# Expert routing by remainders of integer keys, with a running maximum and ids in half precision

## The chip, the cores and the metric

The kernel runs on one core of a Trainium2 chip. The time is that of the device in microseconds (us). The engines are TensorE (PE; its weight loads are PEld), VectorE (DVE), ScalarE (ACT), GpSimd (POOL) and SyncE (SP, which here issues transfers). Each takes its own list of instructions, and a semaphore makes one wait for another. PSUM is the memory that TensorE writes, in eight banks.

## The reference

Three layers follow each other. (1) Attention over windows of 64 positions, 4 batches of 8 heads, 576 positions, head size 64. Its output is x, 2304 tokens of 512. (2) A mixture of 8 experts in which every expert takes exactly 288 tokens:

```
logits = x @ w_gate                       # 2304 x 8
for idx in argsort(-logits.flatten()):    # best (token, expert) pair first
    tok, e = idx // 8, idx % 8
    if assigned[tok] >= 0 or counts[e] >= 288: continue
    assigned[tok] = e; counts[e] += 1
out[mask] = relu(x[mask] @ w1[e]) @ w2[e]  # mask = assigned == e
```

(3) Two dense layers, 512 to 2048 and back, with a leaky relu between them. The result has 2304 rows of 512.

## The kernel before

**Order of the work.** All instructions are issued in program order on each engine; nothing reorders them. attention() runs 18 steps of 128 tokens. Beside it, filler() and ahead() put pieces of other work between the steps. Then Moe.run() goes through experts 0 and 1, the dense layers for the first 512 tokens ("m" 0), experts 2 and 3, "m" 1, and so on. The weights of the dense layers come packed, and Convert unpacks them on ScalarE and VectorE up to the end of "m" 0. RouteDriver.tick() puts routing and conversion pieces between the matmuls: the class Clocks keeps a modelled time for each engine, and a piece is issued when its model says that its inputs are there.

**The routing.** The greedy loop is done in eight phases. In each phase every free token looks at its best open expert, and the phase finds the value at which the first expert becomes full (the threshold). Tokens above it are assigned, and that expert is closed. Its 288 token ids then go to an indirect gather of the rows of x. Phase 0 lies between the end of attention and expert 0; phase p+1 runs beside the work of the experts before it.

**The search in one phase.** A threshold is found in 6 rounds, of 127 candidates (the upper bits of the float32 pattern) and then of 31 (5 bits each). In each round VectorE compares the 18 columns of token maxima m with the candidates T (the grid, GE, in self.G), TensorE counts the hits by expert (18 matmuls of 8 columns into a PSUM tile pc), VectorE compares the counts with what each expert can still take (r_sat), and one matmul with powers of two (pow2) sums the candidates passed. A maximum over experts (r_ns) gives the digit. Then integer instructions put it onto the threshold so far (r_fb) and make the next table of candidates (r_U, r_T). In phase 0, grid and counts are cut into columns 0 to 8 and 9 to 17, and the grid of round 0 has been made by ahead() during attention.

**From threshold to ids.** A scan counts tokens in each expert's order (S), a matmul adds the counts of the other partitions, and each token gets a slot. One-hot tables of slot // 16 (r_OB, three blocks: times column number, times partition number, plain) and slot % 16 (r_lo) are multiplied by 18 matmuls. r_ip spreads the product, and a last float32 product with cf['comb'] gives the ids of 3 x 96 tokens (r_ids). The expert's number (r_eidx) is known earlier, and SP loads its weights with it.

**Where the constants come from.** cft (float32) is loaded on ScalarE's queue at the start, by early(). cbt has two parts: its first 128 columns (an identity) come on ScalarE's queue too; the rest, with the tables tri, iota, cont and spread, is loaded by late() on SP's queue, with cit (integers) ahead of it. late() then calls Router.start(), which sets the routing's state on VectorE.

**PSUM.** attention's pool a_ps has the tags "as" (two buffers of two banks, scores), "apt" and "ao". values() puts the outputs of the last two steps into "as" buffers. After attention the pools m_pa (4 buffers of one bank, tag "acc"), rps (one buffer, all small tiles of the routing), pm and m_ph are opened in this order. The last three steps' outputs are scaled by ScalarE, eight instructions a step (line 185).

Lines: 336 to 339 start(), 354 to 368 ahead(), 137 maxima, 145 exponentials, 152 copies of transposes, 165 values, 1374 and 1375 the loads of late(). Instructions issued after attention all show line 1230, a helper's, so tiles tell them apart.

Of the kernel before, what the change touches and what calls it, by code (L numbers as in the profile page):

```python
# [17 lines left out]
NT = 18  # L18
# [254 lines left out]
U32 = mybir.dt.uint32  # L273
# [3 lines left out]

def consts_np():
# [9 lines left out]
    f['lim'] = np.where(p == 0, -1.0, 3e9).astype(np.float32)  # L288
    f['cid'] = np.broadcast_to(np.arange(18, dtype=np.float32), (128, 18))
    f['pid'] = np.broadcast_to(p, (128, 1))  # L290
# [7 lines left out]
    b['cont'] = np.broadcast_to((np.arange(288) % NT > 0).astype(np.float32), (128, 288))  # L298
    b['spread'] = (j % 6 == np.arange(96) // 16).astype(np.float32)
# [11 lines left out]
class Router:  # L311
# [3 lines left out]
    def __init__(self, nc, pool, pp, L, cf, ci, cb, ones_b, pow2):  # L315
# [6 lines left out]
        self.rem = pool.tile([128, 8], F32, name="r_rem")  # L322
        self.rem0 = pool.tile([128, 8], F32, name="r_rem0")
# [3 lines left out]
        self.OB = pool.tile([128, 1048], BF, name="r_OB")  # L327
        for x in self.G + [self.OB]:
            nc.gpsimd.memset(x, 0.0)
        self.ip = pool.tile([128, 128], F32, name="r_ip")  # L330
    def start(self):
        v, cf = self.nc.vector, self.cf
        v.memset(self.base, 0.0)
        v.memset(self.sat, 0.0)
        v.memset(self.ip, 0.0)
        v.tensor_copy(self.uw, cf['ew'])
        v.memset(self.slotg, 0.0)
        v.memset(self.rem, 288.0)
        v.tensor_scalar(out=self.rem0, in0=self.rem, scalar1=cf['lim'], scalar2=None, op0=ALU.min)
    def ps(self, p, n):  # L340

        self.nps += 1
        return self.pp.tile([128, 128], F32, tag="rp", name=f"rp{self.nps}")[:p, :n]
    def t(self, shape, dt, name, ph):
        bufs = {"fb": 2, "ns": 2, "T": 2, "U": 2, "ids": 8, "eidx": 8}.get(name, 1)
        return self.pool.tile(shape, dt, tag="r_" + name, name=f"r_{name}_{ph}", bufs=bufs)
    def ahead(self, a, b):

        v = self.nc.vector
        if a == 0:  # L350
            self.first = [self.t([128, NT], F32, "m", 0), self.t([128, NT, 8], BF, "oh", 0), self.t([128, NT], F32, "mxw", 0)]
            self.ge0, self.win0 = self.grid(0, 128)
            self.eqw0 = self.G[1].bitcast(F32)[:, :8 * NT].rearrange("p (c e) -> p c e", e=8)
# [15 lines left out]
    def grid(self, k, w):
# [3 lines left out]
    def phase(self, ph, out):  # L373
# [25 lines left out]
        theta = None  # L399
        if ph < 7:  # L400
            fb = ns = U = None
            T = ci['t1']
            for r in range(6):
# [4 lines left out]
                pc = None  # L408
                for lo, hi in () if ph + r == 0 else ((0, 9), (9, 18)) if J > 32 or ph == 0 else ((0, 18),):
                    w = hi - lo  # L410
                    TT(out=GE[:, lo:hi, :J], in0=b3(m[:, lo:hi], w, J), in1=bm(T.bitcast(F32), w, J), op=ALU.is_ge)
                    if hi == 9:
                        yield 'p' if ph == 0 else 'd', 0
                        if ph == 0:
                            pc = self.ps(128, 8)
                            for c in range(9):
                                nc.tensor.matmul(pc, win(c), OH[:, c, :], start=(c == 0), stop=False)
                if r >= 2:
                    nf = t([128, 1], I32, "fb", f"{ph}_{r}")
                    TT(out=nf, in0=fb, in1=ns, op=ALU.bitwise_xor)  # L420
                    fb = nf
                if 1 <= r <= 4:
                    Jn = NB[r]
                    U = t([128, 32], I32, "U", f"{ph}_{r}")
                    TT(out=U[:, :Jn], in0=ci[f'jt{r}'], in1=fb.to_broadcast([128, Jn]), op=ALU.bitwise_xor)
                yield 'p', 0
                c0 = 9 if pc is not None else 0
                pc = self.ps(128, 8) if pc is None else pc
                for c in range(c0, NT):
                    nc.tensor.matmul(pc, win(c), OH[:, c, :], start=(c == 0), stop=(c == NT - 1))  # L430
# [8 lines left out]
                if r == 0:  # L439
                    k = t([128, 2], I32, "k", ph)  # L440
                    TS(out=k[:, 0:1], in0=ns, scalar1=1, scalar2=None, op0=ALU.logical_shift_left)
                    TS(out=k[:, 1:2], in0=k[:, 0:1], scalar1=31, scalar2=0x7FFFFFFF, op0=ALU.arith_shift_right, op1=ALU.bitwise_and)
                    fb = t([128, 1], I32, "fb", f"{ph}_{r}")
                    STT(out=fb, in0=k[:, 0:1], scalar=-1, in1=k[:, 1:2], op0=ALU.bitwise_xor, op1=ALU.bitwise_xor)
                    T = t([128, 31], I32, "T", f"{ph}_{r}")[:, :NB[0]]
                    TT(out=T, in0=ci['jt0'], in1=fb.to_broadcast([128, NB[0]]), op=ALU.bitwise_xor)
                elif r < 5:
                    T = t([128, 31], I32, "T", f"{ph}_{r}")[:, :NB[r]]
                    TT(out=T, in0=U[:, :NB[r]], in1=ns.to_broadcast([128, NB[r]]), op=ALU.bitwise_xor)
                else:  # L450
                    nf = t([128, 1], I32, "fb", f"{ph}_{r}x")
                    TT(out=nf, in0=fb, in1=ns, op=ALU.bitwise_xor)
                    theta = nf.bitcast(F32)
        ge = t([128, 2, NT], F32, "gteq", ph)
        gt, eq = ge[:, 0], ge[:, 1]
        if theta is not None:
            TS(out=gt, in0=m, scalar1=theta, scalar2=None, op0=ALU.is_gt)
            TS(out=eq, in0=m, scalar1=theta, scalar2=None, op0=ALU.is_equal)
# [9 lines left out]
        S = self.OB.bitcast(F32)[:, :16 * NT].rearrange("p (k e c) -> p k e c", k=2, e=8)  # L468
# [947 lines left out]
```

## Time and profile before

| | |
|---|---|
| median of 3 runs | 773.43 us (772.1 to 773.63) |
| the profiled execution's own time | 779.16 us |
| its span, first to last instruction | 777.5 us |
| TensorE busy | 736.7 us (95%) |
| VectorE busy | 448.9 us (58%) |
| ScalarE busy | 335.0 us (43%) |
| GpSimd busy | 169.1 us (22%) |
| DMA | 138.55 MB, mean 178 GB/s |
| mean granted TensorE clock | 0.978 |

In a row of a timeline the first number is the start in us from the span's start, the second the duration, then engine, line, operation, output<-inputs, sizes, and in brackets how long the engine had stood idle and what ended that. TensorE has two clock levels, 1.2 and 2.4 GHz; a granted clock of 1.00 is the upper one. Busy time of PE is no measure of its speed.

### The profile page before, as it was taken

Reading aid. Unit: us, or ns where it says so; the run is one execution under the profiler, and the core shown is the slowest. Engines: PE = TensorE matmul, PEld = TensorE weight load, DVE = VectorE, ACT = ScalarE, POOL = GpSimd, SP = SyncE. Lnnn points to the kernel's source line nnn. Section 1 sums busy time; section 2 is a strip of 40 time slices with the busy share of each in tenths; the row PEclk is TensorE's granted clock in tenths of the full one; section 3 lists DMA queues with packets and bytes.
Section 4 is the critical chain, followed back from the end, with each engine's and each line's share of the span. In section 5 each row is a group of like instructions: output and inputs, shape, how many; then the busy total and the mean of one; then the engine's idle time right before and its main releaser. Section 6 shows DMA issues by size and latency. Waiting matters only on the chain.

```text
span 777.5 us, 15224 instructions
## 1 busy us (share of the span) xinstructions
PE 736.7 (95%) x5872; PEld 625.8 (80%) x5872; DVE 448.9 (58%) x1204; ACT 335.0 (43%) x736; POOL 169.1 (22%) x255
## 2 busy tenths in 40 slices
PE   6999559999999989999999999999999999999996
PEld 4777437798867879997778899988889998888895
DVE  3798778998888978977677324322233222222332
ACT  5898707786645443522112445322244532221321
POOL 5253030400100032120000497200028840000201
PEclk9999769999999999999999999999999999999998
DMA  9996156833883755462144265623436462324752
GB/s 349 408 413 265 46 177 233 299 92 129 265 262 127 254 181 167 138 216 83 55 158 145 81 213 166 220 58 132 163 97 217 152 217 82 108 63 172 253 171 99
DMA packets 39943, 138.55 MB, mean 178 GB/s; under 512 B 4926, under 2 KB 5822, under 8 KB 39872
## 3 DMA queue, kind: packets, MB, share of 16 engines
q1 hardware_dynamic: 35136, 123.19, 45.9%
q0 software_dynamic: 4304, 14.16, 5.3%
q8 instruction: 46, 0.75, 0.4%
q10 hardware_dynamic: 432, 0.25, 0.1%
q14 instruction: 25, 0.20, 0.1%
HBM read 117.65 MB, written 19.92 MB: 177 GB/s over the span
## 4 chain that ended last, share of the span: by engine, by line
PE 83%; DVE 7%; DMA 5%; ACT 2%; issue 1%; another core or an unknown queue 0%; POOLq 0%; POOL 0%; ACTq 0%; SPq 0%; DVEq 0%
PE h L1230 37%; PE oa L1230 24%; PE ya L1230 13%; PE rp L1230 4%; DMA cv_in<-in_wio_dram 2%; PE ao L165 2%; DMA aq<-in_q_dram 1%; DMA avt<-in_vt_dram 1%; PE apt L150 1%; PE xtp L1230 1%; DVE r_G L1230 1%; PE as L130 1%; PE warm L1230 1%; DMA cft<-in_cf_dram 1%; DVE w L1230 1%
## 5 line engine op out<-in xcount | busy, mean ns | idle before, releaser
L1230 PE MATMUL oa<-w,hh 128*128 128x512 f32 x540 | 135.2, 396 | 0.0
L1230 PE MATMUL h<-Y,w 128*128 128x512 f32 (+1 forms) x600 | 134.3, 371 | 0.0
L1230 DVE SCALAR_TENSOR_TENSOR h<-h,tg 128x512 f32<-128x512 f32 (+1 forms) x80 | 51.5, 644 | 133.5 <-ACT tg L1230 131.7
L1230 ACT COPY tg<-h 128x512 f32<-128x512 f32 (+1 forms) x80 | 43.4, 543 | 190.7 <-PE h L1230 185.8
L1230 PEld LDWEIGHTS h<-Y,w 128*128 128x128 f32 x600 | 104.4, 188 | 18.8
L1230 PEld LDWEIGHTS oa<-w,hh 128*128 128x128 f32 x540 | 100.8, 190 | 20.6 <-ACT hh L1230 0.2
L1230 POOL TENSOR_TENSOR w<-raw,w 128x512 fp32r<-128x512 f32 x53 | 66.7, 1292 | 197.1 <-DVE xT L1230 100.8
L1230 PE MATMUL h<-xT,w 128*128 128x288 f32 x672 | 101.5, 299 | 0.0
L1230 PE MATMUL ya<-hh,w 128*128 128x288 f32 x672 | 101.0, 298 | 0.0
L1230 PEld LDWEIGHTS h<-xT,w 128*128 128x128 f32 x672 | 93.2, 189 | 3.0 <-issue 2.4
L1230 PEld LDWEIGHTS ya<-hh,w 128*128 128x128 f32 x672 | 92.8, 190 | 0.3 <-DVE hh L1230 0.2
L1230 PE MATMUL h<-Y,res 128*128 128x512 f32 (+1 forms) x360 | 82.9, 375 | 0.0
L1230 PE MATMUL oa<-res,hh 128*128 128x512 f32 x324 | 82.5, 398 | 0.0
L1230 DVE TENSOR_TENSOR hh<-h,hh 128x512 fp32r<-128x512 f32 (+1 forms) x80 | 50.9, 637 | 38.0 <-ACT hh L1230 37.3
L1230 PEld LDWEIGHTS h<-Y,res 128*128 128x128 f32 x360 | 62.6, 188 | 12.0
L1230 ACT CAST hh<-h 128x512 fp32r<-128x512 f32 (+1 forms) x80 | 43.5, 544 | 64.8 <-DVE h L1230 64.3
L1230 PEld LDWEIGHTS oa<-res,hh 128*128 128x128 f32 x324 | 59.2, 188 | 13.2 <-ACT hh L1230 0.4
L1230 POOL DMA_INDIRECT out_dram<-ot,sidx x18 | 19.2, 1069 | 226.4 <-DVE ot L1230 223.4
L1230 ACT ACTIVATE hh<-h 128x288 fp32r<-128x288 f32 (+1 forms) x64 | 26.5, 414 | 95.3 <-PE h L1230 91.3
L1230 ACT CAST w<-raw 128x512 fp32r<-128x512 f32 x112 | 64.0, 619 | 0.1
L1230 DVE SCALAR_TENSOR_TENSOR hh<-h,hh 128x288 fp32r<-128x288 f32 x56 | 25.4, 453 | 63.9 <-ACT hh L1230 58.9
L145 ACT ACTIVATE ap<-as,anm 128x128 f32<-128x128 f32 x144 | 41.8, 403 | 17.5 <-PE as L130 7.8
(164 smaller groups left out, 933.1 us busy)
## 6 DMA issues: line engine op xcount, KB each, us to landing
w<-wsp SPq DMA_DIRECT2D x80, 512.0 KB, 3.7
raw<-in_w_dram SPq DMA_DIRECT2D x53, 512.0 KB, 3.9
cv_in<-in_wio_dram SPq DMA_DIRECT2D x32, 512.0 KB, 4.4
wsp<-w SPq DMA_DIRECT2D x20, 512.0 KB, 3.1
avo<-in_v_dram SPq DMA_DIRECT2D x6, 876.0 KB, 10.1
aq<-in_q_dram SPq DMA_DIRECT2D x12, 384.0 KB
avt<-in_vt_dram SPq DMA_DIRECT2D x6, 768.0 KB, 9.0
xd<-ax SPq DMA_DIRECT2D x18, 256.0 KB, 7.9
```

What stands on the lines that cost most here:

```text
L130: nc.tensor.matmul(S[64 * t:64 * t + 64, a, u, :].rearrange("p (b c) -> p b c", b=2), q[h], k[h], start=False, stop=True, skip_group_check ...
L145: nc.scalar.activation(p[:, u, :], S[:, a, u, :], AF.Exp, bias=nm[a][:, u:u + 1], scale=0.125)
L150: nc.tensor.transpose(pt[:, u, :], p[:, u, :], ident)
L165: nc.tensor.matmul(o[64 * t:64 * t + 64, h // 4, h % 4, :], ptb[:, u, 64 * t:64 * t + 64], (ve, vo)[t][m][:, s, h, :], start=True, stop=Tr ...
L1230: return f(*a, **kw)
```

## The change

**Keys.** m is turned once a phase into an integer key k that orders like the float (new method keys(); in phase 0 in pieces within ahead()), and k is cut by masks (mk) into six pieces, M. E begins as the first piece (with an offset) plus the second, in float32.

**Rounds.** The candidates are fixed tables (cf['jt0'] to cf['jt4']). The grid compares E minus the digit with them; the digit is read from the PSUM tile of the pow2 product. After the grid one instruction makes the next E: E minus digit plus the next piece. r_T, r_U, r_fb and r_k are gone.

**Full experts.** What an expert can still take is put into the counts by one more matmul (sel times nrem). r_sat is now a scan over the 8 experts, a running maximum cut off at 1, so that column 7 says whether any expert is full, and no maximum over experts is needed.

**Phase 0.** Grid and counts of rounds 1 to 5 are cut into columns 0 to 8, 9 to 14 and 15 to 17, and pc is taken from the pool m_pa (apart).

**Ids.** One block of half-precision numbers: one-hot of slot // 16 times the token number less 1152 (cf['tid']). r_ip and comb are float16. S moves from r_OB to self.G[1]. comb is now a bfloat16 constant of cbt, copied into a float16 tile in start().

The diff, cut to its core:

```diff
 def consts_np():
     for r, (s, n) in enumerate(zip(SHIFTS, NB)):
-        i[f'jt{r}'] = np.broadcast_to((np.arange(1, n + 1) << s).astype(np.int32), (128, n))
+        f[f'jt{r}'] = np.broadcast_to((np.arange(1, n + 1) << s).astype(np.float32), (128, n))
+    i['mk'] = np.broadcast_to(np.array([-1 << 25] + [31 << s for s in SHIFTS], np.int32), (128, 6))
...
+    f['tid'] = 128 * np.arange(18, dtype=np.float32) + p - IDC
-    f['comb'] = (np.where(p < 18, 128, 1) * (j // 6 == np.arange(3))).astype(np.float32)
...
     b['cont'] = np.broadcast_to((np.arange(288) % NT > 0).astype(np.float32), (128, 288))
+    b['comb'] = (j // 6 == np.arange(3)).astype(np.float32)
     b['spread'] = (j % 6 == np.arange(96) // 16).astype(np.float32)
...
     def start(self):
...
-        v.memset(self.rem, 288.0)
-        v.tensor_scalar(out=self.rem0, in0=self.rem, scalar1=cf['lim'], scalar2=None, op0=ALU.min)
-    def ps(self, p, n):
+        v.tensor_scalar(out=self.nrem, in0=self.base[:, 0], scalar1=cf['na'], scalar2=cf['nb'], op0=ALU.mult, op1=ALU.add)
+        v.tensor_copy(self.comb, self.combb)
+    def ps(self, p, n, apart=False):
+        if apart:
+            return self.p0.tile([128, 512], F32, tag="acc", name=f"rq{self.nps}", bufs=4)[:p, :n]
         return self.pp.tile([128, 128], F32, tag="rp", name=f"rp{self.nps}")[:p, :n]
...
+    def keys(self, m, E, a, b, first):
+        if first:
+            v.tensor_scalar(out=z.bitcast(F32), in0=m, scalar1=0.0, scalar2=None, op0=ALU.add)
...
+        v.tensor_scalar(out=k, in0=m, scalar1=31, scalar2=0x7FFFFFFF, op0=ALU.arith_shift_right, op1=ALU.bitwise_and)
+        v.tensor_tensor(out=k, in0=k, in1=m, op=ALU.bitwise_xor)
+        v.tensor_tensor(out=M, in0=k.unsqueeze(1).to_broadcast([128, 6, w]), in1=self.ci['mk'].unsqueeze(2).to_broadcast([128, 6, w]), op=ALU.bitwise_and)
+        v.scalar_tensor_tensor(out=E[:, a:b], in0=M[:, 0], scalar=float(1 << 31), in1=M[:, 1], op0=ALU.add, op1=ALU.add)
...
-                for lo, hi in () if ph + r == 0 else ((0, 9), (9, 18)) if J > 32 or ph == 0 else ((0, 18),):
+                cuts = (0, 18) if ph + r == 0 else (0, 9, 15, 18) if ph == 0 else (0, 9, 18) if r == 0 else (0, 18)
+                for lo, hi in zip(cuts, cuts[1:]):
-                    TT(out=GE[:, lo:hi, :J], in0=b3(m[:, lo:hi], w, J), in1=bm(T.bitcast(F32), w, J), op=ALU.is_ge)
+                    if r:
+                        STT(out=GE[:, lo:hi, :J], in0=b3(E[:, lo:hi], w, J), scalar=dig, in1=bm(cf[f'jt{r - 1}'], w, J), op0=ALU.subtract, op1=ALU.is_ge)
...
+                            if r < 5:
+                                STT(out=En, in0=E, scalar=dig, in1=self.M[:, r + 1], op0=ALU.subtract, op1=ALU.add)
...
+                        pc = self.ps(128, 8, ph == 0)
+                        nc.tensor.matmul(pc, self.sel[r > 0], self.nrem, start=True, stop=False)
...
-                TT(out=self.sat[rows], in0=pc[rows], in1=(self.rem0 if r == 0 else self.rem)[rows], op=ALU.is_ge)
+                v.tensor_tensor_scan(self.sat[rows], pc[rows], self.ones[rows, :8], 0.0, ALU.max, ALU.min)
                 pa = self.ps(128, 8)
                 nc.tensor.matmul(pa, self.pow2[r], self.sat, start=True, stop=True)
+                dig = pa[:, 7:8]
-                ns = t([128, 1], I32, "ns", f"{ph}_{r}")
-                v.tensor_reduce(out=ns, in_=pa, axis=AX.X, op=ALU.max)
...
-            TS(out=gt, in0=m, scalar1=theta, scalar2=None, op0=ALU.is_gt)
+            TS(out=gt, in0=E, scalar1=dig, scalar2=0.0, op0=ALU.subtract, op1=ALU.is_gt)
...
-        TT(out=OB[:, :, 0], in0=OB[:, :, 2], in1=b3(cf['cid'], NT, 18), op=ALU.mult)
-        TS(out=OB[:, :, 1], in0=OB[:, :, 2], scalar1=cf['pid'], scalar2=None, op0=ALU.mult)
...
+        for lo, hi in ((0, 9), (9, 18)) if ph == 0 else ((0, 18),):
+            TT(out=OB[:, lo:hi], in0=HI[:, lo:hi], in1=b3(cf['tid'][:, lo:hi], hi - lo, NT), op=ALU.mult)
...
+            for c in range(lo, hi):
+                nc.tensor.matmul(pi, self.OB[:, NT * c:NT * c + 128], LO[:, c], start=(c == 0), stop=(c == NT - 1))
...
-        nc.tensor.matmul(pj, self.ip, cf['comb'], start=True, stop=True)
+        nc.tensor.matmul(pj, self.ip, self.comb, start=True, stop=True)
...
         pa = ctx.enter_context(tc.tile_pool(name="m_pa", bufs=4, space=PSUM, reuse_waits="tile"))
+        rt.p0 = pa
```

## Rows read from the trace of the kernel before

**Rows 1.** Windows: each engine's busy us (instructions), granted clock, DMA share, GB/s.
```profile
0.00:84.00 84.00, 72.57 (x1503) 57.43 (x1503) 62.17 (x164) 64.14 (x195) 34.56 (x59) 1.00 0.85 333
84.00:107.20 23.20, 6.41 (x122) 4.85 (x123) 17.33 (x78) 10.65 (x31) 1.15 (x2) 0.57 0.16 52
185.00:292.00 107.00, 102.85 (x643) 82.44 (x642) 91.31 (x221) 55.47 (x99) 9.38 (x13) 0.98 0.62 209
```

**Rows 2.** Timeline of VectorE at the start.
```profile
8.33 0.17 DVE L336 COPY r_uw<-cft 128x8 f32<-128x8 f32 x1 [7.00 <-DMA cft<-in_cf_dram]
...
8.57 0.23 DVE L339 TENSOR_SCALAR r_rem<-r_rem,cft 128x8 f32<-128x8 f32 x1
8.71 1.22 DVE L137 TENSOR_REDUCE amx<-as 128x8 f32<-128x1024 f32 x1
```

**Rows 3.** The load of cbt: issue, size, packets from 12.2 to 13.75 and to 15.3.
```profile
6.79 0.43 SPq L1375 DMA_DIRECT2D cbt<-in_cb_dram  x1
...
cbt<-in_cb_dram SPq DMA_DIRECT2D x1, 136.0 KB
...
DMA packets 396, 0.61 MB, mean 394 GB/s; under 512 B 47, under 2 KB 293, under 8 KB 396
...
DMA packets 237, 0.65 MB, mean 422 GB/s; under 512 B 30, under 2 KB 30, under 8 KB 237
```

**Rows 4.** ScalarE's first exponentials; a wait of TensorE (total, times, longest).
```profile
10.23 2.18 ACT L145 ACTIVATE ap<-as,anm 128x128 f32<-128x128 f32 x8 [7.84 <-PE as L130]
...
PE ag L93 <- DMA avt<-in_vt_dram: 0.9, 2, 0.7
```

**Rows 5.** Timelines at the end of attention: TensorE's first counts, ScalarE's scaling.
```profile
83.34 0.53 PE L1230 MATMUL rp<-r_oh,r_G 128*128 128x8 bf16 x15
85.89 0.22 PE L1230 MATMUL rp<-r_oh,r_G 128*128 128x8 bf16 x3 [2.01 <-DVE r_oh L368]
...
84.90 4.98 ACT L185 ACTIVATE ax<-ao,ari 128x64 f32<-128x64 f32 x24
```

**Rows 6.** Timeline of VectorE in the search of phase 0.
```profile
86.14 0.17 DVE L1230 TENSOR_TENSOR r_sat<-rp,r_rem 127x8 bf16<-127x8 f32 x1 [0.31 <-PE rp L1230]
...
87.56 0.81 DVE L1230 TENSOR_TENSOR r_G<-r_m,r_T 128x279 bf16<-128x279 f32 x2
...
91.02 0.17 DVE L1230 TENSOR_TENSOR r_sat<-rp,r_rem 31x8 bf16<-31x8 f32 x1 [0.20 <-PE rp L1230]
91.45 0.17 DVE L1230 TENSOR_REDUCE r_ns<-rp 128x1 int32<-128x8 f32 x1 [0.26 <-PE rp L1230]
...
91.88 0.81 DVE L1230 TENSOR_TENSOR r_G<-r_m,r_T 128x279 bf16<-128x279 f32 x2
...
97.51 0.17 DVE L1230 TENSOR_TENSOR r_sat<-rp,r_rem 31x8 bf16<-31x8 f32 x1 [0.43 <-PE rp L1230]
...
98.33 0.37 DVE L1230 TENSOR_SCALAR r_gteq<-r_m,r_fb_5x 128x18 f32<-128x18 f32 x2
```

**Rows 7.** Timeline of VectorE from threshold to ids in phase 0.
```profile
99.44 0.76 DVE L1230 TENSOR_TENSOR_SCAN r_OB<-cbt,r_G 128x288 f32<-128x288 bf16 x1
...
104.12 0.50 DVE L1230 TENSOR_TENSOR r_OB<-r_hl,cbt 128x324 bf16<-128x324 int32 x1
...
106.36 0.25 DVE L1230 TENSOR_TENSOR r_ip<-rp,cbt 36x96 f32<-36x96 f32 x1 [0.75 <-PE rp L1230]
107.29 0.16 DVE L1230 CAST r_ids<-rp 96x3 int32<-96x3 f32 x1 [0.68 <-PE rp L1230]
```

**Rows 8.** TensorE's waits from 154 to 300; windows behind the two longest.
```profile
PE rp L1230 <- DVE r_sat L1230: 2.4, 1, 2.4
PE rp L1230 <- DVE r_G L1230: 1.8, 1, 1.8
...
220.00:224.50 4.50, 4.50 (x14) 3.35 (x14) 3.98 (x9) 1.90 (x4) 0.00 (x0) 0.62 0.91 304
292.00:296.00 4.00, 4.00 (x27) 3.91 (x28) 2.47 (x8) 1.31 (x3) 1.77 (x3) 0.57 0.85 261
```

More of the change, by code (lines that the diff above doesn't have):

```diff
@@ L276 @@
 FAR = 1.7e38
+IDC = 1152
 def consts_np():
@@ L321, in __init__ @@
         self.slotg = pool.tile([128, NT], F32, name="r_slotg")
-        self.rem = pool.tile([128, 8], F32, name="r_rem")
-        self.rem0 = pool.tile([128, 8], F32, name="r_rem0")
+        self.nrem = pool.tile([128, 8], BF, name="r_nrem")
+        self.sel = [pool.tile([128, 128], BF, name=f"r_sel{k}") for k in range(2)]
+        for k, x in enumerate(self.sel):
+            nc.gpsimd.memset(x, 0.0)
+            for p in range(2):
+                nc.gpsimd.memset(x[32 * p:32 * p + 1, 1 - k:], 1.0)
+        nc.gpsimd.memset(self.sel[0][64:65, 0:1], 1.0)
+        self.comb = pool.tile([128, 3], F16, name="r_comb")
+        self.combb = cb['comb']
+        self.M = pool.tile([128, 6, NT], I32, name="r_M")
+        self.k = pool.tile([128, 2, NT], I32, name="r_k")
         self.spread, self.cont = cb['spread'], cb['cont']
@@ L358, in bm @@
             return ap.unsqueeze(1).to_broadcast([128, b - a, last])
+        ks = self.keys(m, self.e0, a, b, True)
         v.tensor_reduce(out=m, in_=self.Lm[:, a:b], axis=AX.X, op=ALU.max)
@@ L407, in phase @@
                 GE, win = (self.ge0, self.win0) if ph + r == 0 else self.grid(r % 2, jw)
-                pc = None
-                for lo, hi in () if ph + r == 0 else ((0, 9), (9, 18)) if J > 32 or ph == 0 else ((0, 18),):
+                pc, c0 = None, 0
+                cuts = (0, 18) if ph + r == 0 else (0, 9, 15, 18) if ph == 0 else (0, 9, 18) if r == 0 else (0, 18)
+                for lo, hi in zip(cuts, cuts[1:]):
                     w = hi - lo
-                    TT(out=GE[:, lo:hi, :J], in0=b3(m[:, lo:hi], w, J), in1=bm(T.bitcast(F32), w, J), op=ALU.is_ge)
-                    if hi == 9:
-                        yield 'p' if ph == 0 else 'd', 0
[L414 to L427, printed above, removed]
@@ L428, in phase @@
-                pc = self.ps(128, 8) if pc is None else pc
-                for c in range(c0, NT):
-                    nc.tensor.matmul(pc, win(c), OH[:, c, :], start=(c == 0), stop=(c == NT - 1))
+                    if r:
+                        STT(out=GE[:, lo:hi, :J], in0=b3(E[:, lo:hi], w, J), scalar=dig, in1=bm(cf[f'jt{r - 1}'], w, J), op0=ALU.subtract, op1=ALU.is_ge)
+                    elif ph:
+                        TT(out=GE[:, lo:hi, :J], in0=b3(m[:, lo:hi], w, J), in1=bm(ci['t1'].bitcast(F32), w, J), op=ALU.is_ge)
@@ new lines, in phase @@
+                    if hi < NT:
+                        yield 'p' if ph == 0 else 'd', 0
+                    if hi < NT and ph:
+                        continue
+                    if hi == NT:
+                        if r:
+                            En = t([128, NT], F32, "E", f"{ph}_{r}")
+                            if r < 5:
+                                STT(out=En, in0=E, scalar=dig, in1=self.M[:, r + 1], op0=ALU.subtract, op1=ALU.add)
+                            else:
+                                TS(out=En, in0=E, scalar1=dig, scalar2=None, op0=ALU.subtract)
+                            E = En
+                        elif ph:
+                            E = t([128, NT], F32, "E", f"{ph}_0")
+                            for _ in self.keys(m, E, 0, NT, False):
+                                pass
+                        else:
+                            E = self.e0
+                        yield 'p', 0
@@ L431, in phase @@
+                    if pc is None:
+                        pc = self.ps(128, 8, ph == 0)
+                        nc.tensor.matmul(pc, self.sel[r > 0], self.nrem, start=True, stop=False)
+                    for c in range(c0, hi):
+                        nc.tensor.matmul(pc, win(c), OH[:, c, :], start=False, stop=(c == NT - 1))
+                    c0 = hi
                 yield 'v', 1
-                TT(out=self.sat[rows], in0=pc[rows], in1=(self.rem0 if r == 0 else self.rem)[rows], op=ALU.is_ge)
+                v.tensor_tensor_scan(self.sat[rows], pc[rows], self.ones[rows, :8], 0.0, ALU.max, ALU.min)
```

85 lines of the change are left out of this document (41 added, 44 removed).

## The prediction

> **What bounds the kernel now.** Read the windows first [rows 1]. They show a kernel in which TensorE is the limit everywhere but in two places. From 0 to 84 us (attention) TensorE is busy 72.57, VectorE 62.17 and ScalarE 64.14 of 84: a pipeline in which each engine waits a little for the next. From 84 to 107.2 (the search of the first expert, phase 0) TensorE is busy 6.41 of 23.2 and VectorE 17.33: a chain of small instructions, bare, with its clock granted at 0.57. After that TensorE hardly idles: even in 185 to 292, where VectorE is busiest (91.31 of 107), it misses 4.15. So whatever moves the end of attention or the bare chain moves the end of the kernel one for one, and vector work saved in phases 1 to 6 is worth only what TensorE waits for. Then the timelines of VectorE, ScalarE and TensorE, at the start [rows 2 to 4] and around phase 0 [rows 5 to 7], and last TensorE's waits and the windows at half clock in the middle [rows 8].
>
> **The start: a new wait.** start() runs on VectorE ahead of the first scores' maxima. Now it waits for cft alone (the copy at 8.33), and the first maximum starts at 8.71, 0.14 behind the last instruction of start() [rows 2]. The change ends start() with a copy out of cbt['comb']. That constant lies in the part of cbt that late() loads, on SP's queue, issued at 6.79 behind the first q, k, vt and v [rows 3]. When do its rows move? cit and cbt are the only transfers here with rows between 512 B and 2 KB, 128 rows each. From 12.2 to 13.75 the DMA engines handled 293-47 = 246 such packets, from 13.75 to 15.3 none [rows 3]. So cbt lands at about 13.75, and VectorE, which takes its instructions in order, stands from 8.7 to 13.75. Queued behind the copy: the maxima of scores 0 and 1, for which ScalarE's first exponentials wait (10.23 now) [rows 4], for these the transposes, values and the next scores. The first maximum moves from 8.71 to about 13.9: 5.2 later. Nothing gives it back: TensorE's waits for the loads of vt, which the delay hides, are 0.9 in all [rows 4]. I take 5.0, with ends 4.3 (those 0.9 gone) and 5.5 (0.3 between the last packet and the copy). The constants that move from ci to cf lengthen cft and shorten cit; cft is then still there before 13.75, so that costs nothing.
>
> **Keys in attention.** Each of the four groups of ahead() gets five more vector instructions. Two instructions on 18 columns take 0.37 [rows 6], so one costs at most 0.19 and a group 0.9. The first two groups fall where VectorE has little room (62.17 of 84 on the whole [rows 1]); I take a third of their 1.9, 0.6 (ends 0 and 1.9). The last two are covered: by the end of the last values, and by the wait that comes next.
>
> **Phase 0, round 0: a second new wait.** ps(..., apart=True) puts the counts of phase 0 into the pool m_pa instead of rps. m_pa is opened first after attention's pool is closed and takes the first four banks. Those are the banks of attention's tag "as", where by values() the outputs of steps 16 and 17 stand. ScalarE scales them out of PSUM in 24 instructions, 8 a step for 15, 16 and 17, from 84.90, 4.98 us in all, 0.2075 each [rows 5]. Step 16 is done at 84.90+16*0.2075 = 88.22. Now the counts go to another bank: 15 matmuls at 83.34, the last 3 at 85.89, r_sat at 86.14 [rows 5, 6]. After the change the first matmul of round 0 waits for 88.22, and then 19 follow (15 took 0.53, so 0.67 and some 0.1 to r_sat): r_sat at 89.0, 2.85 later. If the bank is one of step 17 it is 84.90+4.98 = 89.88, and 4.5 later; with no such wait 0.3 later (the keys). I take 2.85.
>
> **Phase 0, the search.** From r_sat to the next grid round 0 takes 87.56-86.14 = 1.42 [rows 6]: maximum, four instructions on the key, table. After the change the grid reads the digit straight from PSUM: what is left is r_sat to r_ns, 91.45-91.02 = 0.43. That saves 0.99. In each of rounds 1 to 4 the maximum and the table go, 91.88-91.45 = 0.43: 1.72. Round 5 ends with 98.33-97.51 = 0.82, after it 0.43: 0.39. From grid to r_sat it is now 2.16-0.86 = 1.30, where 2.16 is a third of 97.51-91.02. Three pieces (9, 6, 3 columns) in place of two (0.81 for both) cost about 0.06 more on VectorE and leave 3 matmuls behind the last one instead of 9, at 0.035 each 0.2 less, of which TensorE's backlog of the earlier pieces eats some; I take 0.1 a round, 0.5 in five. Sum 3.6.
>
> Two prices are not shown. The scan on 8 columns lies between the compare it replaces, 0.17, and the scan on 288 columns, 0.76 [rows 6, 7]; I take 0.17, as the width is that of the compare. At the other end six scans cost 3.5 more. The Trainium skill (DVE: opcode table, instruction layouts, handler registers and perf-mode slots, Datapath and trigger behaviour) says that a scan runs at half throughput, so its price goes by columns; by that rule 8 columns add next to nothing and the low end holds. A scalar read from PSUM by the grids: an 8-column copy out of SBUF took 0.17 [rows 2] and an 8-column compare out of PSUM 0.17 [rows 6], so I take nothing. The Trainium skill (VectorE: DVE Perf Modes, The TRN2 errata) gives a PSUM source 120 fixed cycles against 58; by that an estimate of 0.065 for each of 15 pieces, 1.0 in all against this change; the two rows don't show it.
>
> **Phase 0, ids.** From 104.12 to r_ip at 106.36, four wide instructions and 18 matmuls [rows 7]. After: two compares, then the products in two halves, the first 9 matmuls under the second half; by the same widths 0.3 less. From r_ip to r_ids 107.29-106.36 = 0.93, of which 0.25 is r_ip: 0.68 for a float32 product. A half-precision one should take what the r_sat product takes, 0.43-0.17 = 0.26: 0.42 less. Sum 0.7 (ends 0.3 and 1.0). Phase 0 is thus 2.85-3.6-0.7 = 1.45 shorter, and the gathers and weights that its ids and eidx start move with it.
>
> **Later phases.** A round in phases 1 to 6 loses about 0.5 of vector time (maximum, table, two updates against one new one), the keys give 0.7 back: some 3 us a phase, under TensorE's work. The added count matmul of 36 rounds at 0.035 is 1.3 on TensorE, seven float32 products less give about that back. TensorE's large waits there are 1.8 for r_G and 2.4 for r_sat, and the clock behind them: granted 0.62 in 4.5 us and 0.57 in 4.0 (the 1.2 GHz level for most of it, after the idling), each losing 1.7 [rows 8]. A planner orders the instructions by modelled times, so changed lengths deal these waits anew: all 7.6 can go, or one more of 3.5 can come. I take 0.5 less.
>
> **Sum.** 5.0 + 0.6 - 1.45 - 0.5 = +3.65 on the profiled execution, 779.16 (span 777.5 and 1.66 around it). That one lies 5.73 over the median of three, 773.43; nothing in the sum depends on that, so 777.1.
>
> **Rivals.**
> 1. The relief decides: VectorE's 3 us a phase come early enough that both stalls of rows 8 go, 7.6 instead of 0.5: 3.65+0.5-7.6 = -3.45, 770.0. For: VectorE is busy 85% there. Against: the grid of the first stall has nothing of routing queued ahead that the change shortens, and the keys come on top. It decides once more than 4.15 of the 7.6 are gone. 0.13.
> 2. No bank wait (another place, or the scaling is over by then): 0.3 for 2.85, +1.1, 774.5. For: the banks are read from the order of the pools, not from a row. Against: m_pa comes first and four banks is what "as" had. 0.14.
> 3. The late start is swallowed because loads, not engines, pace attention: +3.65-5.0 = -1.35, 772.1. For: DMA share 0.85 over the 84 us [rows 1]. Against: TensorE's waits for loads after the start are 0.9. Also the case that the copy doesn't wait. 0.10.
> 4. A new stall of TensorE in the re-dealt order, 1.8 and 1.7 of clock: +3.65+3.5, 780.6. 0.11.
>
> **How the numbers follow.** The forecast has 0.52 and its own range is 775.0 to 779.5 (start 4.3 to 5.5, keys 0 to 1.9, later ±2). The range 771.0 to 780.5 leaves out most of rival 1 and half of rival 4. What a measurement here can tell from no change is 0.2%, 1.55: 771.9 to 775.0. Slower: nearly all of the forecast, rival 4 and some of rival 2, 0.63. Same: most of rival 2, half of 3 and the forecast's low edge, 0.19. Faster: rival 1, the rest of 3, 0.18.
>
> **What would show it.** The start: the first maximum at 13.9 with VectorE idle ahead of it until cbt's load; at 8.9 the first step is wrong, and with it the forecast. The bank: TensorE's first count matmul waiting for ScalarE's ax until 88.2 plus the shift. The search: rounds of about 1.64 instead of 2.16, r_sat to grid 0.43. The ids: 0.26 in place of 0.68. Later: two waits of TensorE near 218 and 290, or not.

## The result, and the profile after

The changed kernel takes 780.77 us (median of 4 runs, 779.68 to 781.95); the kernel before took 773.45 beside it (4 runs). The ratio is 1.0099 [1.0077, 1.0121]: 7.3 us slower. The forecast had the sign, the new wait of VectorE and half the size: +3.65, range up to 780.5.

The profiled execution took 781.95 (span 780.3). Its windows (span, then busy us and count of PE, PEld, VectorE, ScalarE, GpSimd, then granted clock, DMA share, GB/s), attention first and last the stretch in which routing runs beside the experts:

```profile
0.00:84.00 84.00, 70.23 (x1380) 54.68 (x1382) 57.15 (x153) 58.76 (x180) 33.90 (x64) 0.96 0.86 330
193.00:300.00 107.00, 105.59 (x708) 83.99 (x709) 94.24 (x219) 63.44 (x116) 4.78 (x14) 1.00 0.60 208
```

Against [rows 1], the first 84 us hold 123 matmuls less and the clock is 0.96 instead of 1.00. The later stretch (moved by 8 us, about the shift; it holds more matmuls than before, 708 for 643) misses 1.41 of TensorE instead of 4.15. And from r_ids, the last step of phase 0, to the last instruction it is 780.3-115.15 = 665.2 us here and 772.6-107.84 = 664.8 in a second profile of the kernel before (before_again). So the loss lies ahead of r_ids, and it begins at the start. VectorE there (start, duration, engine, line, operation, in brackets idle time and releaser):

```profile
8.50 0.72 DVE L349 TENSOR_SCALAR r_nrem<-r_base,cft 128x8 bf16<-128x8 f32 x1
...
14.13 0.17 DVE L350 CAST r_comb<-cbt 128x3 f16<-128x3 bf16 x1 [4.91 <-DMA cbt<-in_cb_dram]
14.21 1.22 DVE L137 TENSOR_REDUCE amx<-as 128x8 f32<-128x1024 f32 x1
```

The copy waits for cbt as forecast, and the first maximum starts at 14.21, 5.5 later than in [rows 2]. What the forecast had not seen stands on TensorE:

```profile
16.15 1.25 PE L150 MATMUL apt<-cft,ap 128*128 128x128 f32 x4 [3.89 <-ACT ap L145]
...
19.16 1.12 PE L150 MATMUL apt<-cft,ap 128*128 128x128 f32 x4
20.20 0.64 PE L121 MATMUL as<-maskb,cbt 64*64 64x512 bf16 x4
```

and in the windows behind that wait:

```profile
14.00:16.00 2.00, 0.00 (x0) 0.00 (x0) 1.84 (x4) 0.27 (x2) 0.00 (x0) 1.00 1.05 422
16.00:18.00 2.00, 1.25 (x4) 0.73 (x4) 0.93 (x2) 2.00 (x9) 0.00 (x0) 0.54 1.02 411
18.00:20.00 2.00, 1.68 (x16) 1.44 (x16) 0.36 (x1) 0.75 (x2) 0.30 (x1) 0.50 1.04 427
20.00:24.00 4.00, 4.00 (x71) 3.19 (x70) 1.26 (x2) 2.66 (x9) 3.71 (x6) 0.63 1.03 410
```

TensorE stood idle for 3.89 us and came back at the lower level: 0.54, 0.50, 0.63. In the kernel before, these four windows are granted 1.00, and the masks of a step (line 121, x4) take 0.41 where they take 0.64 here. TensorE and the last two windows there:

```profile
13.91 0.41 PE L121 MATMUL as<-maskb,cbt 64*64 64x512 bf16 x4
...
18.00:20.00 2.00, 1.77 (x44) 0.94 (x38) 1.46 (x2) 2.00 (x8) 0.14 (x1) 1.00 1.03 424
20.00:24.00 4.00, 4.00 (x102) 3.51 (x98) 2.44 (x7) 3.56 (x12) 0.00 (x0) 1.00 1.02 406
```

A good mark for the progress of attention is VectorE's line 176, which sums the products for the gate once a step ("the sums" from here on). The sums of step 0, before and after:

```profile
17.37 0.27 DVE L176 TENSOR_REDUCE L<-al 128x8 f32<-128x64 f32 x1
```

```profile
24.73 0.27 DVE L176 TENSOR_REDUCE L<-al 128x8 f32<-128x64 f32 x1
```

So the shift grows from 5.5 at the first maximum to 24.73-17.37 = 7.4 at the sums of step 0. At the end of attention it is still there:

```profile
92.40 1.89 ACT L185 ACTIVATE ax<-ao,ari 128x64 f32<-128x64 f32 x9
```

The scaling begins at 92.40 instead of 84.90 [rows 5], 7.5 later (its 24 instructions appear here in several rows). Phase 0 then begins with the second forecast wait, TensorE on ScalarE's ax, and its rounds on VectorE look like this:

```profile
95.77 0.17 PE L1262 MATMUL rq<-r_nrem,r_sel 128*128 128x8 bf16 x1 [4.83 <-ACT ax L185]
```

```profile
96.46 0.17 DVE L1262 TENSOR_TENSOR_SCAN r_sat<-rq,ones 127x8 bf16<-127x8 f32 x1 [2.86 <-PE rq L1262]
96.89 1.07 DVE L1262 SCALAR_TENSOR_TENSOR r_G<-r_E,rp,cft 128x279 bf16<-128x279 f32 x3 [0.26 <-PE rp L1262]
97.88 0.23 DVE L1262 SCALAR_TENSOR_TENSOR r_E<-r_E,rp,r_M 128x18 f32<-128x18 f32 x1
98.31 0.18 DVE L1262 TENSOR_TENSOR_SCAN r_sat<-rq,ones 31x8 bf16<-31x8 f32 x1 [0.19 <-PE rq L1262]
...
106.14 0.38 DVE L1262 TENSOR_SCALAR r_gteq<-r_E,rp 128x18 f32<-128x18 f32 x2 [0.26 <-PE rp L1262]
...
112.05 0.46 DVE L1262 TENSOR_TENSOR r_lo<-r_hl,cbt 128x288 f16<-128x288 int32 x1
112.43 0.49 DVE L1262 TENSOR_TENSOR r_G<-r_hl,cbt 128x324 f16<-128x324 int32 x1
112.95 0.33 DVE L1262 TENSOR_TENSOR r_OB<-r_G,cft 128x162 f16<-128x162 f16 x1
113.79 0.33 DVE L1262 TENSOR_TENSOR r_OB<-r_G,cft 128x162 f16<-128x162 f16 x1 [0.51 <-PE rp L1262]
...
115.15 0.16 DVE L1262 TENSOR_SCALAR r_ids<-rp 96x3 int32<-96x3 f32 x1 [0.28 <-PE rp L1262]
```

The first scan is at 96.46, that is 88.96 plus the 7.5 of attention: the forecast's 89.0. A round takes 98.31-96.46 = 1.85, not 1.64. From the first r_sat to r_gteq it is 9.68 instead of 98.33-86.14 = 12.19 [rows 6]: 2.51 saved where 3.6 were forecast. From 112.05 to r_ids it is 3.10 instead of 107.29-104.12 = 3.17 [rows 7]: 0.07 saved where 0.7 were.

The profiled execution is only 2.8 longer than the one before, because that one was itself long: before_again (774.21) has the wait for r_G near 220 again, but not the one for r_sat at 289 of [rows 8], which came in one of the two executions, the one on which the sum was made.

```profile
220.05 0.38 PE L1230 MATMUL rp<-r_oh,r_G 128*128 128x8 bf16 x9 [1.75 <-DVE r_G L1230]
```

### The profile page after: what moved, and what is told of

Read it like the earlier page. It is cut to its first block, busy times and chain, and to the rows that moved or that the text cites. A ratio compares the mean times of both kernels' runs of the same rounds, so it can differ in the third digit from the quotient of the medians.

```text
span 780.3 us, 15243 instructions
## 1 busy us (share of the span) xinstructions
PE 735.5 (94%) x5906; PEld 624.5 (80%) x5906; DVE 438.3 (56%) x1113; ACT 334.8 (43%) x736; POOL 173.2 (22%) x262
## 4 chain that ended last, share of the span: by engine, by line
PE 74%; DVE 17%; DMA 4%; ACT 3%; issue 2%; POOLq 0%; SPq 0%; POOL 0%; DVEq 0%; ACTq 0%
PE h L1262 33%; PE oa L1262 21%; PE ya L1262 10%; DVE r_G L1262 3%; PE rp L1262 3%; DVE w L1262 2%; PE ao L165 2%; DMA cv_in<-in_wio_dram 2%; PE apt L150 1%; DVE cv_r L1262 1%; PE as L130 1%; DVE amx L137 1%; PE xtp L1262 1%; DMA cbt<-in_cb_dram 1%; DVE hh L1262 1%
## 5 line engine op out<-in xcount | busy, mean ns | idle before, releaser
L1262 PE MATMUL oa<-w,hh 128*128 128x512 f32 x540 | 132.9, 392 | 0.0
L1262 PE MATMUL oa<-res,hh 128*128 128x512 f32 x324 | 80.6, 393 | 0.0
L145 ACT ACTIVATE ap<-as,anm 128x128 f32<-128x128 f32 x144 | 41.6, 396 | 24.3 <-DVE anm L138 16.8
```

The costliest lines, as they stand in the source:

```text
L145: nc.scalar.activation(p[:, u, :], S[:, a, u, :], AF.Exp, bias=nm[a][:, u:u + 1], scale=0.125)
L1262: return f(*a, **kw)
```

## The experiments

Each kernel is compared with the kernel before on its own chip, beside it. There were four series, each on one chip: comb_late, before_stall, comb_late_pm and before_again; stall_warm, pm_cut2, pm_ids_whole and pm_dig_sbuf; after_again, stall_warm_again, late_pm_again and late_pm_whole; stall_busy and stall_tiny. From series to series the kernel before moves between 772.66 and 777.75, so ratios, not times, go across them.

**before_again: the kernel before once more.**

> The kernel before, once more, for a second profile. Its profiled execution took 779.16 against a median of 773.43. If the two stalls of TensorE near 218 and 289 us belong to that execution alone, the second profile lacks one or both and its span is some 4 to 6 shorter; if they belong to the program, both are there again.

Measured: 772.36, ratio to itself 0.9981 [0.9964, 0.9999]. So a difference of 0.2% between two kernels is about what no change gives. Of the two stalls the profile has one, near 220.

**comb_late: the copy moved out of the start.**

```diff
 def start(self):
-        v.tensor_copy(self.comb, self.combb)
 def ahead(self, a, b):
         if a == 0:
+            v.tensor_copy(self.comb, self.combb)
```

> The changed kernel with one instruction moved: the copy of comb leaves start() and becomes the first instruction of ahead(), at step 5 of attention. Theory A (the copy stops VectorE until 14.1 us, and the idle TensorE then restarts at the lower clock, 7.5 us by the end of attention): about 7.4 less than the changed kernel, 773.4 us, first maximum at 8.9, end of the scaling by ScalarE (line 185) back near 90. Rival B (the copy costs only its own 5.5 us, the other 2 come from the keys in attention): 775.3. Rival C (attention would have swallowed the start, the loss lies in phase 0 and later): near 780.

Measured: 773.6, ratio 0.9999 [0.9985, 1.0013]. The 1% is gone: step 2 starts at 14.15, the sums of step 0 come at 17.61, the scaling starts at 85.49, and ids come at 108.24 instead of 115.15.

```profile
17.61 0.27 DVE L176 TENSOR_REDUCE L<-al 128x8 f32<-128x64 f32 x1
...
85.49 4.98 ACT L185 ACTIVATE ax<-ao,ari 128x64 f32<-128x64 f32 x24
...
108.24 0.16 DVE L1262 TENSOR_SCALAR r_ids<-rp 96x3 int32<-96x3 f32 x1 [0.28 <-PE rp L1262]
```

The place of a copy of 128x3 elements is worth 6.9 us at ids and 1.0% of the time.

**before_stall: the wait alone, in the kernel before.** One copy out of the late part of cbt at the end of start(), nothing else of the change.

```diff
+        v.tensor_copy(self.comb, self.tri[:, :3])
```

> The kernel before with one instruction added: start() ends with a copy of three columns of tri, a table in the same late part of cbt. Nothing else of the change. Theory A: 7.3 more than before, 780.7, with the second step's scores at 20.2 instead of 13.9. Rival B: 5.5 more, 778.9. Rival C: within 1 of 773.4.

Measured: 782.46, ratio 1.0108 [1.0088, 1.0129]. The same wait and the same slow restart:

```profile
14.32 0.17 DVE L341 COPY r_comb<-cbt 128x3 bf16<-128x3 bf16 x1 [5.30 <-DMA cbt<-in_cb_dram]
```

```profile
16.34 1.25 PE L150 MATMUL apt<-cft,ap 128*128 128x128 f32 x4 [4.04 <-ACT ap L145]
```

So one instruction accounts for the whole loss; nothing of the new search is needed for it.

**comb_late_pm: no wait for the bank.** comb_late, with the counts of phase 0 in the bank of pool pm, which no output of the last steps holds.

```diff
-            return self.p0.tile([128, 512], F32, tag="acc", ..., bufs=4)[:p, :n]
+            return self.p0.tile([128, 512], F32, tag="xt", ..., bufs=1)[:p, :n]
...
-        rt.p0 = pa
         pm = ...
+        rt.p0 = pm
```

> comb_late with the counts of phase 0 in the pool pm (the bank that attention's tag apt held) instead of m_pa. Theory A (the first count matmul waits for ScalarE's scaling of step 16, 2.85 us): the wait is gone, r_sat of round 0 some 2.5 earlier, 770.9 us, and the time of the whole follows. Rival D (the wait is only the visible end of another chain, so something else is late in its place): less than 1 below comb_late.

Measured: 771.23, ratio 0.9969 [0.9957, 0.998]; repeated on another chip (late_pm_again) 0.9982 [0.997, 0.9995]. The first scan is at 86.57 with 0.22 of idle time ahead of it, ids at 105.25.

```profile
85.16 4.96 ACT L185 ACTIVATE ax<-ao,ari 128x64 f32<-128x64 f32 x24
...
86.57 0.17 DVE L1262 TENSOR_TENSOR_SCAN r_sat<-rq,ones 127x8 bf16<-127x8 f32 x1 [0.22 <-PE rq L1262]
...
105.25 0.16 DVE L1262 TENSOR_SCALAR r_ids<-rp 96x3 int32<-96x3 f32 x1 [0.28 <-PE rp L1262]
```

From the scaling's start to ids it is 20.09 us, against 22.75 in comb_late and 22.39 before: the bank wait costs 2.66 (forecast 2.85), and without it the new phase 0 is 2.30 shorter than the old one. This version is clearly faster than the changed kernel. Against the kernel before it is 0.31% and 0.18% faster; the second is no more than what the kernel before differed from itself (0.19%), so a gain of about 2 us in time is likely, as the 2.30 have it, but not shown beyond doubt.

**stall_warm: keep TensorE busy in the wait.** The changed kernel with 16 matmuls whose result nobody reads.

```diff
             if i == 1:
                 stage_g(0)
+                dummy = pp.tile([128, 2, 512], F32, tag="ao", name="dummy", bufs=1)
+                for n in range(16):
+                    nc.tensor.matmul(dummy[:, n % 2], identb, maskb, start=True, stop=True)
```

> The changed kernel with 16 matmuls of 512 columns added (their result is never read) behind the gate product of step 0, where TensorE waits 3.89 us for the first exponentials. Theory A (of the 7.4 us by which attention ends later, 5.5 are the wait for cbt and the rest is the clock, granted at 0.50 to 0.77 from 14 to 24 us because TensorE idled): the granted clock stays 1.00 from 14 to 24, the masks of step 2 take 0.41 instead of 0.64, step 2 starts at about 19.0 instead of 20.2, step 4 at about 27.1 instead of 29.1, ScalarE's scaling at about 90.5 instead of 92.4, and the time is about 1.9 below the changed kernel's 780.8: 778.9. Rival B (the slower clock is hidden behind ScalarE and VectorE, and the 1.9 come from the order in which they take their work after the wait): clock up, but scaling at 92.4 and 780.8.

Measured: ratio 1.0099 [1.0081, 1.0117], the changed kernel's own. The clock stayed at 1.00, and the sums of step 0 came at 22.7 instead of 24.7; but from step 4 on TensorE had waits of 0.6 to 1.3 that the profile gives no releaser for, and the scaling began at 93.3. Neither theory describes that: the time is rival B's, the late waits are nobody's. Beside after_again on one chip:

> The changed kernel as it is, for comparison with the one below on the same chip. Step 2 of the scores at 20.2, the sums of step 3 at about 36.3, ScalarE's scaling at about 92.4, ratio to the kernel before 1.010.

> The 16 matmuls in TensorE's wait once more, beside the changed kernel on one chip. In their first run the clock stayed 1.00 and the sums of steps 0 to 3 came 2.0 to 2.3 us earlier than in the changed kernel's trace, but at steps 4, 5 and 10 TensorE waited for what no engine explains, and the end of attention was 0.9 later. Theory A (those waits were of that execution; the clock costs about 2 us): scaling at about 90.4, 2 us below the run beside it in time, ratio about 1.0075. Rival B (whatever the clock gives back at the start, later waits take it again: attention is held by its loads): waits at steps 4, 5 and 10 again, scaling within 0.7 of the run beside it, the same time.

Measured: after_again 1.0116 [1.0094, 1.0138], scaling at 92.67; stall_warm_again 1.0118 [1.0091, 1.0145], with sums of step 0 at 24.3, as the clock fell in this execution too (0.89 from 18 to 20, 0.63 from 20 to 24), one such wait near step 4 (0.9), a longer one behind ScalarE's conversion (3.0), and the scaling only at 96.28. Inconclusive: the clock was not held in the profiled execution, and the added instructions had a price of their own. Its four runs point at the clock all the same: 784.87 and 785.83 us with a mean granted clock of 0.980 and 0.981, 788.37 and 788.60 with 0.977 and 0.976. The next pair gives both kernels the same instructions.

**stall_busy and stall_tiny: same instructions, other work.** Twenty more matmuls at the same places, 16 ahead of the first transposes, 4 behind them; they differ only in columns.

```diff
-                    nc.tensor.matmul(dummy[:, n % 2, :512], identb, maskb[:, :512], start=True, stop=True)
+                    nc.tensor.matmul(dummy[:, n % 2, :8], identb, maskb[:, :8], start=True, stop=True)
```

> The changed kernel with 20 matmuls of 512 columns in TensorE's waits at the start, 16 ahead of the first transposes and 4 behind them. Granted clock 1.00 from 14 to 24 us, sums of step 0 at 22.7. Theory A (the lower clock costs 2 us of time): 2 us below stall_tiny at step 0, at the end of attention and in the time. Rival B (attention is held later by something else, so that what the clock gives back is waited away): 2 us below stall_tiny at step 0, within 0.7 of it at the end of attention, and the same time.

> The same 20 instructions with 8 columns each: TensorE is as good as idle in the wait. Clock at 0.5 to 0.8 from 14 to 24 us, sums of step 0 at 24.7 to 25.0. Theory A: time 2 us above stall_busy. If the later waits at steps 4, 5 and 10 come with the number of instructions, they stand here too and the time is above the changed kernel's by what they take, 1.5 to 3; if they come with the earlier steps, they are gone here.

Measured, on one chip: stall_busy 781.36, ratio 1.0112 [1.0094, 1.0129]; stall_tiny 783.63, ratio 1.0142 [1.0124, 1.0161]. Their windows, stall_busy first:

```profile
16.00:18.00 2.00, 1.65 (x8) 0.86 (x8) 1.27 (x2) 1.93 (x8) 0.00 (x0) 1.00 1.02 404
18.00:20.00 2.00, 1.79 (x23) 1.03 (x24) 0.36 (x1) 1.23 (x4) 0.29 (x1) 1.00 1.00 412
20.00:24.00 4.00, 4.00 (x104) 3.50 (x100) 2.67 (x7) 3.81 (x14) 3.74 (x6) 1.00 1.03 414
```

```profile
16.00:18.00 2.00, 1.34 (x8) 0.88 (x8) 0.78 (x2) 2.00 (x9) 0.00 (x0) 0.59 1.01 402
18.00:20.00 2.00, 1.82 (x16) 1.44 (x16) 0.36 (x1) 0.62 (x2) 0.44 (x1) 0.50 1.01 417
20.00:24.00 4.00, 4.00 (x70) 3.33 (x70) 1.40 (x2) 2.66 (x9) 3.58 (x6) 0.60 1.03 411
```

The sums of step 0, again stall_busy first:

```profile
23.23 0.27 DVE L176 TENSOR_REDUCE L<-al 128x8 f32<-128x64 f32 x1
```

```profile
24.71 0.27 DVE L176 TENSOR_REDUCE L<-al 128x8 f32<-128x64 f32 x1
```

The programs differ in those columns alone, and the granted clock with them. The difference is 1.5 at the sums of step 0, 1.3 at the scaling (93.41 against 94.73) and 783.63-781.36 = 2.3 in time. In stall_busy's profile cbt landed later (its copy is at 14.47, stall_tiny's at 13.98); counted from the copy it is 2.0 at the sums and 1.8 at the scaling. Theory A holds, and rival B, with the same time, falls. The size is less sure than the sign: the intervals of the two ratios just overlap, because one of stall_busy's six runs took 783.63. That run had a mean granted clock of 0.978, the other five (780.4 to 781.73) 0.981 to 0.983. Both kernels have the unexplained waits, so these come with the instructions and not with the earlier steps. TensorE's waits from 28 to 75 us (total, times, longest), stall_busy and then stall_tiny:

```profile
PE as L130 <- issue: 2.5, 2, 1.4
```

```profile
PE as L130 <- issue: 2.7, 2, 1.6
```

In the changed kernel the only such wait there is 0.2. "issue" names no releaser; why twenty instructions at 12 to 18 us bring waits from 37 us on stays open.

**pm_dig_sbuf: the digit from SBUF.** comb_late_pm with one more copy a round in phase 0, so that the grids read their scalar in SBUF instead of PSUM.

```diff
                 dig = pa[:, 7:8]
                 yield 'v', 0
+                if ph == 0:
+                    dg = t([128, 1], F32, "dg", f"{ph}_{r}")
+                    v.tensor_copy(dg, dig)
+                    dig = dg
```

> comb_late_pm, in phase 0 with the digit copied from PSUM into SBUF by one more vector instruction a round, and the grids reading it there. Theory A (a scalar operand in PSUM costs each instruction 0.067 more): the three pieces of a grid take 0.87 instead of 1.07, the update of E 0.17 instead of 0.23, and the copy costs 0.15 to 0.2, so a round is 1.75 to 1.85. Rival B (the three-operand instruction is slower than the two-operand one wherever the scalar stands): grids of 1.07 stay, and a round is 1.85+0.17 = 2.0.

Run once, for its rows; its time is not compared. Measured, in its second round:

```profile
89.77 0.18 DVE L1266 TENSOR_TENSOR_SCAN r_sat<-rq,ones 31x8 bf16<-31x8 f32 x1 [0.18 <-PE rq L1266]
90.21 0.16 DVE L1266 COPY r_dg<-rp 128x1 f32<-128x1 f32 x1 [0.26 <-PE rp L1266]
90.40 1.06 DVE L1266 SCALAR_TENSOR_TENSOR r_G<-r_E,r_dg,cft 128x279 bf16<-128x279 f32 x3
91.38 0.23 DVE L1266 SCALAR_TENSOR_TENSOR r_E<-r_E,r_dg,r_M 128x18 f32<-128x18 f32 x1
91.80 0.18 DVE L1266 TENSOR_TENSOR_SCAN r_sat<-rq,ones 31x8 bf16<-31x8 f32 x1 [0.20 <-PE rq L1266]
```

The grids take 1.06 as before, the update of E 0.23, and a round is 2.03: theory A falls. Nor is it the three-operand form. In the trace after, on 18 columns:

```profile
103.44 0.23 DVE L1262 SCALAR_TENSOR_TENSOR r_E<-r_E,rp,r_M 128x18 f32<-128x18 f32 x1
...
105.29 0.23 DVE L1262 TENSOR_SCALAR r_E<-r_E,rp 128x18 f32<-128x18 f32 x1
...
108.14 0.17 DVE L1262 TENSOR_SCALAR r_mxw<-r_mxw 128x18 f32<-128x18 f32 x1
...
110.62 0.18 DVE L1262 SCALAR_TENSOR_TENSOR r_ac<-r_self,r_gteq 128x18 f32<-128x18 f32 x1
```

Two operands or three, with a scalar written into the instruction it is 0.17 and 0.18; with one read from a tile it is 0.23 for both forms. The price, 0.05 to 0.07 an instruction, is that of a scalar that stands in a tile, whichever memory holds it. It stood in the trace before: r_loc, whose scalar is a tile, took 0.23 there, and r_mxw 0.17. Nor does it grow with the columns: a whole grid of 558 columns in phase 1 takes 0.81 in comb_late and 0.74 in the kernel before. (r_nrem at the start, with two such scalars and 0.72, prices something else: in stall_busy the same instruction took 0.42. What held it is not shown.)

**pm_cut2: two pieces a grid.** comb_late_pm with cuts (0, 9, 18) in phase 0.

> comb_late_pm with the grids of phase 0 in two pieces (9, 9 columns) instead of three (9, 6, 3). Theory A (a piece costs the fixed part of an instruction, and the matmuls of the last piece are what the scan waits for): the grids take 1.07-0.22 = 0.85 instead of 1.07, but 9 matmuls instead of 3 follow the last one, 0.2 more: rounds of 1.80 to 1.87 instead of 1.85, the time within 0.3 of comb_late_pm's 771.2. Rival B (TensorE's backlog of 6 matmuls behind the second piece already eats what the third piece saves): rounds of 1.70, 0.7 less in five rounds, 770.5.

Measured: rounds of 1.87 (89.36 to 91.23), the grids 0.94:

```profile
89.79 0.94 DVE L1262 SCALAR_TENSOR_TENSOR r_G<-r_E,rp,cft 128x279 bf16<-128x279 f32 x2 [0.26 <-PE rp L1262]
```

Theory A holds for the round, though the grids were to take 0.85: the third piece costs VectorE 0.13, and buys 0.02 a round. Two pieces take 0.94 where the kernel before took 0.81 [rows 6], 0.065 a piece for the scalar. One round of the five took 2.64, with VectorE waiting 1.07 for TensorE; pm_ids_whole, with three pieces, has such a round too (1.00), so this is not the cut's, and its cause is open. The ratio is 0.9995 [0.9981, 1.0009], on another chip than comb_late_pm's 0.9969 and 0.9982; this close to what no change gives (0.0019) it doesn't decide.

**pm_ids_whole: the ids' product in one piece.** comb_late_pm with

```diff
-        for lo, hi in ((0, 9), (9, 18)) if ph == 0 else ((0, 18),):
+        for lo, hi in ((0, 18),):
```

> comb_late_pm with the product of the ids' block in one piece of 18 columns instead of two of 9. Theory A (the second half's write overlaps the windows that the first 9 matmuls read, so the halves run one behind the other and the split only adds 0.5 of wait): no wait of VectorE for TensorE ahead of the block, from the first product to r_ip 1.67 becomes about 0.6+0.2+0.8 = 1.5 to 1.3, the time 0.2 to 0.4 below comb_late_pm's 771.2: 770.9. Rival B (the matmuls under the second half are worth as much as the wait): the same, 771.2.

and once more beside comb_late_pm on one chip:

> comb_late_pm as it is, for comparison with the one below on the same chip: ratio to the kernel before 0.997, ids 2.7 us after the compare of the block's rows begins.

> pm_ids_whole beside comb_late_pm on one chip. Theory A (the split costs VectorE a wait of 0.5 and gives back less): 0.4 us less from the compare to ids, as its first trace showed (2.28 for 2.71), and 0.4 less in time, ratio 0.9964 beside 0.9969. Rival B (gathers and weights, not the ids, release the first expert's matmuls): the same time.

Measured: 0.9989 [0.9974, 1.0004], then late_pm_whole 0.9978 [0.9961, 0.9995] beside late_pm_again's 0.9982 [0.997, 0.9995]. From the compare r_G (slot // 16) to ids it is 2.29 (103.14 to 105.43) instead of 2.72 (103.50 to 106.22): 0.43 of the chain saved, as theory A has it, but no difference in time that these runs can show, so on what the 0.43 is worth they don't decide.

## Why the forecast missed

The sum missed by 7.3-3.65 = 3.7 us, about half of it in each of two places: the start (1.9) and phase 0 (1.8, of which 1.1 in the search and 0.6 in the ids).

**The first step that failed: the start, 5.0 us.** "Nothing gives it back: TensorE's waits for the loads of vt, which the delay hides, are 0.9 in all [rows 4]. I take 5.0, with ends 4.3 (those 0.9 gone) and 5.5 (0.3 between the last packet and the copy)." This counts the wait on VectorE and what could give it back, and stops there. Measured at ids, the copy's place costs 6.9 (after against comb_late); by the ratios of these two it is 1.0% or 7.7 us, with before_stall 1.08% or 8.4. About 5 of it is the wait: with the clock held, the sums of step 0 come 22.7-17.6 = 5.1 later in stall_warm than in comb_late. About 2 are the clock (2.0 at the sums and 2.3 in time by the pair stall_busy and stall_tiny). Its ends were ends of the wait alone. The rows to see it were on the page: [rows 1] has a granted clock of 0.57 where TensorE idles, [rows 8] prices a restart after 1.8 and 2.4 us of idling at 1.7 each, and rival 4 added exactly that to a new wait. The forecast used it in the middle of the kernel and forgot it at the start, because the new wait was VectorE's. But behind VectorE's wait stood a wait of 3.89 of TensorE. The Trainium skill (TensorE: Matmul & The Clock Gate, HAM oscillation — how this bites in real kernels) says that a TensorE kept waiting for loads starts its next work cold; here it did so with a vector instruction in between, at the 0.50 of these rows.

**The bank wait: right.** Forecast 2.85 and 89.0; measured 2.66, and 88.96 after the shift. Reading the order of the pools as an order of banks was enough; rival 2 is out.

**The second step that failed: the search, 3.6 us, of which 2.51 came.** r_sat to grid went from 1.42 to 0.43 in round 0 and from 0.86 to 0.43 in the others, as forecast; the scan on 8 columns took 0.17 to 0.18. Grid to r_sat is 98.31-96.89 = 1.42 where 1.30 was measured before and 1.20 forecast. Both halves of that term failed: the third piece saves 0.02 and not 0.1, and each piece costs 0.07 for its scalar, which I had taken at nothing. The estimate of 1.0 that the forecast worked out from the Trainium skill (VectorE: DVE Perf Modes, The TRN2 errata) and set aside has the right size by a reason that does not hold here: that page gives a price for reading PSUM, and pm_dig_sbuf shows the same 1.06 with nothing read from PSUM. So its agreement is no support for the rule; the two rows that spoke against it (8 columns out of SBUF and out of PSUM, 0.17 each) were read rightly, but neither had a scalar in a tile.

**The third: the ids, 0.07 instead of 0.7.** The half-precision product does save what was forecast (VectorE waits 0.28 for it, 0.68 before [rows 7]). The split gives it back: the second half's product waits 0.51 for TensorE. Its columns begin at 162, and the windows of 128 columns that the first nine matmuls read reach over them. The forecast put these matmuls under the second half without asking what they read. Without the split the ids come 0.43 earlier (late_pm_whole), so one piece would have saved 0.50; the remaining 0.2 of the forecast, taken from the widths, did not come.

**Keys and later phases.** Keys: without the late start the scaling begins at 85.49 (comb_late) and 85.16 (comb_late_pm), while the kernel before itself has 84.90 and, in before_again, 85.43. So the keys cost 0 to 0.6 and can't be told from nothing; 0.6 was forecast. Phase 0 from scaling to ids: +0.36 (22.75 against 22.39) instead of -1.45. Later phases: 7.3 in all less 6.9, 0.36 and the keys leaves 0 to -0.6, with the ratio's interval of 1.7 on either side; -0.5 was forecast. Rival 1 had a part: TensorE's longest wait from 154 to 300 is 0.9 in the trace after, but of the two stalls it counted, one recurs in the kernel before and the other doesn't, so there was less to win than its 7.6. Rival 3 is the reverse of what happened: nothing swallowed the late start, and TensorE's clock added to it.

So 6.9 + 0.36 = 7.3, and nothing that these runs can measure is left for keys and later phases.

## What to carry to other kernels

A wait added to one engine is priced on every engine that it makes idle: follow it to TensorE, read how long TensorE will stand there, and add what the restart at the lower clock costs (here 2 us on a wait of 5). When setup code is moved or extended, ask of each of its instructions which load it touches and what is queued behind it. A scalar operand has a price by its kind, written into the instruction or read from a tile; compare rows that differ in that alone.

## What the runs showed of the hardware

- A scalar read from a tile costs a vector instruction 0.05 to 0.07 us, alike from PSUM and SBUF and with two or three operands (0.23 against 0.17 and 0.18 on 18 columns).
- After TensorE's wait of 3.89 the windows from 16 to 24 us were granted 0.50 to 0.63. With 20 matmuls of 512 columns in the wait they were granted 1.00 (stall_busy), with 20 of 8 columns 0.50 to 0.60 (stall_tiny), and the times lie 2.3 us apart. Sixteen of 512 columns held it in one profile (stall_warm) and not in another (stall_warm_again, 0.63 from 20 to 24).
- With twenty extra matmuls at 12 to 18 us TensorE had waits of 2.5 to 2.7 in all from 37 us on that name no releaser, where the changed kernel had 0.2. The ratio of stall_tiny, 1.0142, is above the changed kernel's 1.0099 and 1.0116 by about as much; that the waits cause this is likely, not shown.
